# Slot 2 scored in one fp32 product from q and k as loaded, with a new list of steps

## The chip, the cores and the metric

The kernel runs on one core of one Trainium2 chip. The metric is the device time of one execution in microseconds (us). A core has TensorE (PE in the profile; its weight loads are PEld), VectorE (DVE), ScalarE (ACT), GpSimd (POOL) and SyncE (SP), which here issues every DMA.

## The reference

Two layers. The first is attention over 8 batches, 8 heads, 576 positions and head size 64, with a bias that falls with the running sum of `s`; the second is a mixture of 4 attention experts, of which each position takes the 2 with the largest gate.

```python
scores = scale * q @ k.T                       # per batch and head
cum = cumsum(maximum(s, 0))
scores = where(causal, -1e9, scores + minimum(-(cum_q - cum_k), 0))
attn = softmax(scores);  x = attn @ v          # heads side by side: x is [8, 576, 512]
logits = x @ w_gate                            # the top 2 of 4 experts, softmax of the two logits
for e in range(4):
    a = softmax(causal(scale * (x @ wq[e]) @ (x @ wk[e]).T))
    out += gate[e] * (a @ (x @ wv[e]) @ wo[e])
```

## The kernel before

The work is cut into slots numbered 0 to 49; a slot is one pair of heads (first layer) or one pair of experts (second layer) of one batch. Slots 0 to 3 are the four pairs of heads of batch 0. The keys of a slot lie on the partitions of the score banks and the queries on the columns, so each slot computes transposed scores `p[k, q]` for two heads.

Steps of a slot n, by the letters of the list (the number before the colon in the list is the slot at which the step is registered, so that a step on slot n's inputs stands under n-1 or n-2):

- `ld` loads q and k of a pair to a tile `raw` (L566, L576 for v as `lv`). `h0`..`h3` (L670, L674, ACT) copy them to fp32r tiles Q2 and K2; `lq`, `lk` make second copies (L689 POOL and L698 ACT in the first slots, DMAs later); `l0`..`l3` (L705, L711, DVE) store what the rounding to fp32r left over. `hc` (L632, L663) puts the running sums into rows 64 and following of the keys.
- `m0`..`m5` (L730, PE) compute a bf16 version of the scores, `M0`..`M5` (L744, DVE) reduce it to a row maximum per query; `M4` is the last. `mt` (L764, PE) turns the maxima, `mA` (L768, ACT) negates them, `mq` (L773, two DMAs, one for each head) writes them as row 96 of the queries. After that row has landed the true scores can be taken: the product itself subtracts the maximum.
- `s0`..`s6` are the scores (PE), `E0`..`E6` the exponentials (ACT), `b` the causal edges and `d` the sums (POOL), `v` the product with v (PE, L908), `a` and `r` the denominators, `n`, `N`, `o` the normalisation, `p` the projections of the second layer (PE, L1138).

An ordinary slot needs two fp32r products for each piece of its scores: the first with the rounding remainders (K1 and Q1, L798), the second with the rounded values, the sums and the maxima (K2 and Q2, L803). The slots in `DIRECT` (0 and 1) take another way: q and k are loaded by DMA into a tile `plain` without any rounding (`h0`, `h1`, L635 and L636), the rows beside them are set by memsets (`z0`, `z1` on DVE, `z2`, `z3` on POOL), and each piece is one fp32 product (L792, the tail L830), which the trace shows as two instructions. These slots need no `ld`, no `h2`, `h3` and no `l` steps.

The order on every engine is written out by hand in `ORDER` (L64), a list of 3951 steps; nothing moves at run time except by waiting. All DMAs go through SP's queue in that order. The list also has 60 spare products `i` (L1381): bf16 matmuls on a tile of zeros, whose results nobody reads. Forty of them stand at the very start of PE and twenty between the turn of slot 0's maxima (`-1:mt`) and slot 0's first scores.

Of the kernel before, what the change touches and what calls it, by code (L numbers as in the profile page):

```python
# [8 lines left out]
F32 = mybir.dt.float32  # L9
# [30 lines left out]
def pieces(kt, q0, q1):  # L40
# [302 lines left out]
def tile_attention_then_moe(ctx, tc, qk, vm, vt, s, wqk, wvg, wo, out):  # L343
# [244 lines left out]
    def r2(n):  # L588
        return n % NQK2
# [895 lines left out]
```

## Time and profile before

| | |
|---|---|
| median of 3 runs | 652.89 us (650.82 to 654.0) |
| the profiled execution | 653.66 us |
| its span, first to last instruction | 651.9 us |
| PE busy | 639.9 us, 98% of the span |
| DVE, ACT, POOL busy | 514.0, 467.4, 414.4 us |
| mean granted TensorE clock | 0.988 of full speed |

The page gives one execution. "Busy" is the time in which an engine has an instruction in work; matmuls overlap, so the start of the next matters more than the length of one. A granted clock of 1.00 stands for 2.4 GHz and 0.50 for 1.2 GHz.

### The profile page before, as it was taken

The page shows a single profiled execution, that of the slowest core. Times are in us where ns is not written, and L with a number is a line of the kernel's source. Part 1 is how long each engine was busy: PE and PEld are TensorE (multiplying, and loading weights), DVE is VectorE, ACT ScalarE, POOL GpSimd, SP SyncE. Part 2 cuts the span into 40 slices and gives each one's busy share as a digit, 9 for nine tenths or more (in the row PEclk, how much of TensorE's full clock was granted, in tenths as well). Part 3 has the DMA queues.
Part 4 walks back from the last instruction along what each step waited for, and adds up shares of the span by engine and source line. Part 5 has one row for each costly group of instructions (what it writes and reads, how often), then busy time and mean ns, then how long its engine had stood idle before and what let it go on. Part 6 is the DMA issues. An engine that isn't in the chain of part 4 may idle for free.

```text
span 651.9 us, 16521 instructions
## 1 busy us (share of the span) xinstructions
PE 639.9 (98%) x5891; PEld 529.3 (81%) x5891; DVE 514.0 (79%) x1459; ACT 467.4 (72%) x1077; POOL 414.4 (64%) x558
## 2 busy tenths in 40 slices
PE   7999999999999999999999999999999999999997
PEld 3377798888887898888888888878987888889875
DVE  7587978996888768988778788888778867874894
ACT  5268978777768767777677767777587866576564
POOL 9298567676756585675594758638765669837030
PEclk9699999999999999999999999999999999999999
DMA  7433553452547446264464346553445725232313
GB/s 169 138 111 102 154 144 103 134 136 62 148 112 182 104 129 170 72 179 140 125 170 136 120 95 166 146 145 109 112 129 157 203 61 129 59 110 73 95 45 114
DMA packets 49559, 81.29 MB, mean 125 GB/s; under 512 B 19892, under 2 KB 19892, under 8 KB 49478
## 3 DMA queue, kind: packets, MB, share of 16 engines
q1 hardware_dynamic: 49478, 80.24, 46.4%
q8 instruction: 47, 0.77, 0.5%
q14 instruction: 34, 0.28, 0.1%
HBM read 44.61 MB, written 10.16 MB: 84 GB/s over the span
## 4 chain that ended last, share of the span: by engine, by line
PE 92%; DMA 3%; ACT 2%; DVE 1%; SPq 1%; issue 1%; ACTq 0%; DVEq 0%
PE pvp L908 20%; PE pq L1138 16%; PE s L798 11%; PE s L803 10%; PE mx L730 10%; PE pw L1138 9%; PE po L1138 7%; PE sm L961 4%; DMA raw<-in_qk_dram 2%; PE s L792 2%; PE i L1381 1%; PE s L839 1%; PE po L1112 1%; PE mt L764 1%; ACT p L819 1%
## 5 line engine op out<-in xcount | busy, mean ns | idle before, releaser
L744 DVE CUSTOM_DVE_ANT_0 sink<-mx,mask 128x64 bf16<-128x64 f32 (+7 forms) x432 | 169.5, 428 | 56.2 <-PE mx L730 41.4
L819 ACT ACTIVATE p<-s 128x512 f32<-128x512 f32 x288 | 160.4, 593 | 52.1 <-PE s L803 40.0
L851 POOL TENSOR_SCALAR_AFFINE_SELECT p<-p 128x256 f32<-128x256 f32 (+1 forms) x192 | 95.4, 506 | 142.0 <-ACT p L819 117.0
L798 PE MATMUL s<-q,k 128*128 128x320 f32 (+2 forms) x552 | 149.7, 297 | 0.0
L803 PE MATMUL s<-q,k 97*128 97x320 f32 (+2 forms) x552 | 141.4, 290 | 1.3 <-DMA q<-mr 1.3
L872 POOL TENSOR_TENSOR r<-r,p 128x640 f32<-128x640 f32 (+1 forms) x92 | 128.6, 1399 | 4.3
L798 PEld LDWEIGHTS s<-q,k 128*128 128x128 f32 x552 | 105.0, 190 | 7.8 <-issue 4.0
L803 PEld LDWEIGHTS s<-q,k 97*128 97x128 f32 x552 | 105.0, 190 | 2.2 <-DMA q<-mr 1.5
L1138 PE MATMUL pq<-x,wqkh 128*128 128x288 f32 x512 | 106.2, 300 | 0.0
L908 PE MATMUL pvp<-p,v 128*64 128x128 f32 (+3 forms) x1024 | 99.9, 321 | 0.0
L705 DVE TENSOR_TENSOR q<-raw,q 64x576 fp32r<-64x576 f32 x92 | 78.7, 870 | 25.2 <-ACT q L670 9.0
L711 DVE TENSOR_TENSOR k<-raw,k 64x1024 fp32r<-64x1024 f32 (+1 forms) x92 | 82.7, 913 | 13.7 <-PE s L798 6.0
L730 PE MATMUL mx<-k,q 96*64 96x512 bf16 (+7 forms) x920 | 86.3, 293 | 1.0 <-ACT p L844 1.0
L1138 PEld LDWEIGHTS pq<-x,wqkh 128*128 128x128 f32 x512 | 81.5, 188 | 2.5 <-ACT pv L922 1.0
L908 PEld LDWEIGHTS pvp<-p,v 128*64 128x64 f32 x1024 | 63.7, 136 | 23.3 <-issue 3.0
L1138 PE MATMUL pq<-x,wqkl 128*128 128x288 f32 x256 | 75.5, 295 | 0.0
L670 ACT ACTIVATE q<-raw 64x576 fp32r<-64x576 f32 x92 | 62.0, 678 | 6.3 <-DMA raw<-in_qk_dram 5.1
L674 ACT ACTIVATE k<-raw 64x128 fp32r<-64x128 f32 (+1 forms) x92 | 61.8, 680 | 5.2 <-DMA raw<-in_qk_dram 3.1
L730 PEld LDWEIGHTS <-q 96*64 96x64 bf16 x920 | 45.0, 110 | 19.7 <-issue 6.2
L867 POOL TENSOR_TENSOR r<-p 128x256 f32<-128x256 f32 x46 | 37.4, 812 | 34.1 <-ACT p L819 34.1
L869 POOL TENSOR_TENSOR r<-p 128x384 f32<-128x384 f32 x46 | 49.2, 1070 | 11.3 <-ACT p L819 11.2
L922 ACT ACTIVATE pv<-pvp 128x256 f32<-128x256 f32 (+1 forms) x92 | 36.5, 402 | 25.4 <-PE pvp L908 25.1
(146 smaller groups left out, 1162.8 us busy)
## 6 DMA issues: line engine op xcount, KB each, us to landing
raw<-in_qk_dram SPq DMA_DIRECT2D x30, 576.0 KB
rb<-rr SPq DMA_DIRECT2D x92, 144.0 KB
q<-q SPq DMA_DIRECT2D x45, 288.0 KB
k<-k SPq DMA_DIRECT2D x39, 288.0 KB
v<-in_vm_dram SPq DMA_DIRECT2D x32, 256.0 KB
out_dram<-o SPq DMA_DIRECT2D x32, 256.0 KB
q<-mr SPq DMA_DIRECT2D x92, 2.2 KB
plain<-in_qk_dram SPq DMA_DIRECT2D x4, 288.0 KB
```

The lines of the kernel that those rows point to most:

```text
L670: nc.scalar.activation(q2[0:64, j], get_raw(n)[0:64, j], AF.Copy)
L705: nc.vector.tensor_tensor(a[64:128, j], get_raw(n)[0:64, j], q2[0:64, j].bitcast(F32), op=OP.subtract)
L711: nc.vector.tensor_tensor(part(c[0:64]), get_raw(n)[64:128, :, k], part(c[64:128]).bitcast(F32), op=OP.subtract)
L730: nc.tensor.matmul(t[64 * j : 64 * j + 64, c0 : c0 + k1 - k0], q2[0:RC, 64 * qt : 64 * qt + 64], keys(n, RC, j, k0, k1).bitcast(BF16)[:, 1 ...
L744: nc.vector.tensor_tensor_reduce(sink[:, c0 : c0 + w], t[:, c0 : c0 + w], mask[:, m0 : m0 + w], scale=1.0, scalar=mcol[n][:, 9:10] if bi = ...
L798: nc.tensor.matmul(t[0:nk, c0 : c0 + q1 - q0], K1[r1(n)][:, span(j, k0, k0 + nk)], Q1[r1(n)][:, j, q0:q1], start=True, stop=False,)
L803: nc.tensor.matmul(t[0:nk, c0 : c0 + q1 - q0], K2[r2(n)][0 : RM + 1, span(j, k0, k0 + nk)], Q2[r2(n)][0 : RM + 1, j, q0:q1], start=False, ...
L819: nc.scalar.activation(ptile[n][:, x % 2, 512 * ci : 512 * ci + 512], tl[x], AF.Exp, scale=0.125)
L851: nc.gpsimd.affine_select(out=a if kt else running()[:, :, 0:128], in_=a, pattern=[[64 if kt == 4 else 0, 2], [1, nk]], compare_op=OP.is_g ...
L872: add(r[:, :, q0:S], r[:, :, q0:S], p[:, :, 1024 + c : 1024 + c + S - q0], op=OP.add)
L908: nc.tensor.matmul(cur[h][64 * j : 64 * j + 64, q0 - PVC[h] : q1 - PVC[h]], vsl(j, kt), rtile[n][:, j, 0:128] if own else ptile[n][:, j, c ...
L1138: nc.tensor.matmul(t[0:nk, 0:w], l, r, start=(x == 0), stop=(x == len(terms) - 1))
```

## The change

`DIRECT` grows from (0, 1) to (0, 1, 2). Slot 2's q and k get a tile each, of the tag `raw2`: the two buffers in which later the projections leave the experts' q and k. Its `hc` copies the sums from the early table in SBUF instead of the table in DRAM. Nine steps go (`-1:ld`; `0:h2`, `0:h3`; `1:lq`, `1:lk`, `1:l0` to `1:l3`), four memsets come (`0:z0` to `0:z3`), and `0:h0`, `0:h1` turn from ACT copies into DMAs.

```diff
-DIRECT = (0, 1)
+DIRECT = (0, 1, 2)
...
     def whole(n):
-        if n not in plain:
+        if n not in plain and n < 2:
             w = sb.tile([P, 2, 4, S], F32, tag="x", name="plain", bufs=1)
-            for x, m in enumerate(DIRECT):
-                plain[m] = w[:, x]
+            for m in range(2):
+                plain[m] = w[:, m, 0:2], w[:, m, 2:4]
+        elif n not in plain:
+            plain[n] = tuple(
+                sb.tile([P, 2, S], F32, tag="raw2", name=f"plain{x}", bufs=2) for x in "qk"
+            )
         return plain[n]
...
-                nc.sync.dma_start(whole(n)[64:66, 2 + j], early[0][hd : hd + 1, 0:2])
+                nc.sync.dma_start(whole(n)[1][64:66, j], early[0][hd : hd + 1, 0:2])
...
-        items["h0"] = lambda: nc.sync.dma_start(whole(n)[0:64, 0:2], heads[0:64])
-        items["h1"] = lambda: nc.sync.dma_start(whole(n)[0:64, 2:4], heads[64:128])
+        items["h0"] = lambda: nc.sync.dma_start(whole(n)[0][0:64], heads[0:64])
+        items["h1"] = lambda: nc.sync.dma_start(whole(n)[1][0:64], heads[64:128])
```

The memsets and the other readers of the tile change their indices in the same way. The list itself is new throughout: of the 3942 steps that both lists have, the longest common run in order has 958. The start of both lists, cut to the steps of one engine (`i x40` for forty spare products):

```
PE before   i x40 | -2:m0 -2:m1 -2:m2 -1:m5 -1:m3 0:m5 0:m3 0:m4 -1:m0 -1:m1 -1:m2 -1:m4 -1:mt | i x20 | 0:s5 0:s4 ...
PE after    i x40 | -2:m0 -1:m3 -2:m2 -2:m1 -1:m1 0:m3 -1:m5 -1:m0 0:m5 0:m4 -1:m4 -1:m2 i -1:mt | i x19 | 0:s0 0:s1 ...
DVE before  -2:z1 -2:z0 -1:z0 -2:c2 -2:c3 2:l2 -2:c4 2:l0 -2:M0 -2:M1 -2:M2 -1:M5 -1:M3 -1:M4 ...
DVE after   -1:z0 -2:z1 -1:z1 -2:c2 -2:c3 -2:c4 0:z1 2:w0l -2:z0 -2:M0 -2:M1 -2:M2 -1:M5 -1:M3 -1:M4 ...
ACT before  1:h2 -2:c1 1:h0 2:lk 0:h3 0:h2 1:lk 0:h1 0:h0 2:w0h -1:mA ...
ACT after   -2:c1 2:w0h 2:lk 5:w0h 1:h2 2:h2 2:h3 2:h1 -1:mA ...
SP before   0:ld -2:c0 -2:h1 -1:h0 -2:h0 -1:ld -2:hc -1:h1 -1:hc 2:w0f -2:cu 1:ld -1:mq ...
SP after    -2:c0 -1:h0 2:w0f -2:h1 5:w0f -2:h0 0:ld -1:hc -2:hc -1:h1 1:ld -2:cu 0:hc 0:h0 2:ld 3:w0f -1:mq ...
```

Here `c0` loads `s`, `c1` to `c4` make the running sums (`c1` on ACT, the scan `c2` and the splits `c3`, `c4` on DVE), `cu` stores them to DRAM with four DMAs, and `w0f`, `w0h`, `w0l` load a weight and split it.

## Rows read from the trace of the kernel before

**Rows 1.** The page's head: the span, the busy times of the engines, and the shares of the engines in the chain that ended last.

```profile
span 651.9 us, 16521 instructions
PE 639.9 (98%) x5891; PEld 529.3 (81%) x5891; DVE 514.0 (79%) x1459; ACT 467.4 (72%) x1077; POOL 414.4 (64%) x558
PE 92%; DMA 3%; ACT 2%; DVE 1%; SPq 1%; issue 1%; ACTq 0%; DVEq 0%
```

**Rows 2.** All waits of PE from 60 us to the end (waiting line, releaser, us in total, times, longest).

```profile
PE mx L730 <- ACT p L844: 1.0, 1, 1.0
PE sm L1059 <- DVE r L872: 0.3, 1, 0.3
```

**Rows 3.** PE's timeline of the first 60 us: start, length, line, operation, count, and in brackets the idle time before it.

```profile
1.35 10.72 PE L1381 MATMUL i<-sink 128*128 128x512 bf16 x40 [1.35 <-DVE sink L373]
12.60 0.36 PE L730 MATMUL mx<-plain 96*64 96x448 bf16 x1 [0.53 <-DVE p L473]
13.25 1.23 PE L730 MATMUL mx<-plain 96*64 96x448 bf16 x17 [0.29 <-DMA plain<-p]
16.33 3.04 PE L730 MATMUL mx<-plain 96*64 96x256 bf16 x22 [1.86 <-DMA w_qk<-in_wqk_dram]
20.32 0.37 PE L764 MATMUL mt<-ident,mcol 128*9 128x128 f32 x1 [0.94 <-DVE mcol L744]
20.48 9.52 PE L1381 MATMUL i<-sink 128*128 128x512 bf16 x20
29.89 5.60 PE L792 MATMUL s<-plain 128*128 128x320 f32 x24
35.33 0.27 PE L764 MATMUL mt<-ident,mcol 128*9 128x128 f32 x1
...
38.36 3.72 PE L792 MATMUL s<-plain 128*128 128x256 f32 x16
...
47.23 0.42 PE L798 MATMUL s<-q,k 128*128 128x320 f32 x1
...
50.38 0.34 PE L839 MATMUL s<-q,k 128*128 128x128 f32 x2
50.65 0.43 PE L730 MATMUL mx<-k,q 96*64 96x320 bf16 x4
...
56.67 0.31 PE L798 MATMUL s<-q,k 128*128 128x320 f32 x1
58.30 0.42 PE L803 MATMUL s<-q,k 97*128 97x320 f32 x1 [1.31 <-DMA q<-mr]
```

**Rows 4.** Windows of the start: from and to in us, their length, busy us (and instructions) of PE, PEld, DVE, ACT, POOL, the granted clock, the DMA engines' busy share and GB/s.

```profile
5.00:10.00 5.00, 5.00 (x24) 2.23 (x23) 2.72 (x4) 3.17 (x5) 4.70 (x18) 1.00 1.04 204
...
14.00:15.00 1.00, 0.47 (x8) 0.16 (x2) 1.00 (x5) 0.99 (x3) 0.87 (x3) 1.00 0.69 237
15.00:16.00 1.00, 0.00 (x0) 0.00 (x0) 1.00 (x9) 0.99 (x2) 1.00 (x2) 0.75 0.59 194
...
25.00:29.00 4.00, 3.99 (x10) 1.43 (x10) 0.32 (x1) 0.00 (x0) 0.00 (x0) 0.50 0.76 236
```

**Rows 5.** DVE's timeline of the start (columns as in rows 3): the running sums and their two splits, the first and the last maxima of slot 0.

```profile
7.32 1.35 DVE L457 TENSOR_TENSOR_SCAN s_c<-s_r 64x576 f32<-64x576 f32 x1 [2.21 <-ACT s_r L452]
8.70 1.05 DVE L463 TENSOR_SCALAR p<-s_c 64x576 int32<-64x576 int32 x1
9.78 0.75 DVE L469 TENSOR_TENSOR p<-s_c,p 64x576 f32<-64x576 f32 x1
...
11.84 0.75 DVE L473 TENSOR_TENSOR p<-p 64x576 f32<-64x576 f32 x1
...
13.79 0.62 DVE L744 CUSTOM_DVE_ANT_0 sink<-mx,mask 128x448 bf16<-128x448 f32 x1 [0.42 <-POOL plain L640]
...
16.69 0.69 DVE L744 CUSTOM_DVE_ANT_0 sink<-mx,mask 128x512 bf16<-128x512 f32 x1
...
19.41 0.75 DVE L744 CUSTOM_DVE_ANT_0 sink<-mx,mask,mcol 128x512 bf16<-128x512 f32 x1 [2.02 <-PE mx L730]
```

**Rows 6.** SP's issues in the same stretch (start, time that the issuing took, line, transfer, count).

```profile
2.62 1.26 SPq L635 DMA_DIRECT2D plain<-in_qk_dram  x2
...
10.63 1.45 SPq L632 DMA_DIRECT2D plain<-p  x2
12.13 0.67 SPq L636 DMA_DIRECT2D plain<-in_qk_dram  x1
...
21.01 1.64 SPq L773 DMA_DIRECT2D plain<-mr  x2
```

**Rows 7.** The chain that ended last, in order of time: two of its DMA pieces (start, length).

```profile
0.81 5.10 DMA raw<-in_qk_dram
...
54.33 3.92 DMA q<-mr
```

**Rows 8.** Groups of instructions of the first 60 us (count, busy us, mean ns of one, idle time before them).

```profile
L711 DVE TENSOR_TENSOR k<-raw,k 64x1024 fp32r<-64x1024 f32 (+1 forms) x6 | 5.6, 958 | 0.1
L670 ACT ACTIVATE q<-raw 64x576 fp32r<-64x576 f32 x8 | 5.4, 676 | 3.9 <-DMA raw<-in_qk_dram 3.8
...
L705 DVE TENSOR_TENSOR q<-raw,q 64x576 fp32r<-64x576 f32 x6 | 4.7, 786 | 0.2
...
L638 DVE MEMSET plain<- 32x1152 f32 x2 | 2.0, 1018 | 0.6 <-DVE q L705 0.3 <-issue 0.3
```

More of the change, by code (lines that the diff above doesn't have):

```diff
@@ L608, in whole @@
     def whole(n):
-        if n not in plain:
+        if n not in plain and n < 2:
             w = sb.tile([P, 2, 4, S], F32, tag="x", name="plain", bufs=1)
-            for x, m in enumerate(DIRECT):
-                plain[m] = w[:, x]
+            for m in range(2):
[4 more added lines that the diff above has]
+            )
         return plain[n]
     def queries(n):
-        return whole(n)[:, 0:2] if n in DIRECT else Q2[r2(n)]
+        return whole(n)[0] if n in DIRECT else Q2[r2(n)]
     def keys(n, rows, j, k0, k1):
         if n in DIRECT:
-            return whole(n)[0:rows, 2 + j, k0:k1]
+            return whole(n)[1][0:rows, j, k0:k1]
         return K2[r2(n)][0:rows, span(j, k0, k1)]
@@ L631, in sums_in @@
                 hd = 2 * i + j
-                nc.sync.dma_start(whole(n)[64:66, 2 + j], early[0][hd : hd + 1, 0:2])
+                nc.sync.dma_start(whole(n)[1][64:66, j], early[0][hd : hd + 1, 0:2])
         items["hc"] = sums_in
-        items["h0"] = lambda: nc.sync.dma_start(whole(n)[0:64, 0:2], heads[0:64])
-        items["h1"] = lambda: nc.sync.dma_start(whole(n)[0:64, 2:4], heads[64:128])
-        items["z0"] = lambda: nc.vector.memset(whole(n)[64:96, 0:2], 1.0)
-        items["z1"] = lambda: nc.vector.memset(whole(n)[96:128, 0:2], 0.0)
-        items["z2"] = lambda: nc.gpsimd.memset(whole(n)[64:96, 2:4], 0.0)
-        items["z3"] = lambda: nc.gpsimd.memset(whole(n)[96:128, 2:4], 1.0)
+        items["h0"] = lambda: nc.sync.dma_start(whole(n)[0][0:64], heads[0:64])
+        items["h1"] = lambda: nc.sync.dma_start(whole(n)[1][0:64], heads[64:128])
+        items["z0"] = lambda: nc.vector.memset(whole(n)[0][64:96], 1.0)
+        items["z1"] = lambda: nc.vector.memset(whole(n)[0][96:128], 0.0)
+        items["z2"] = lambda: nc.gpsimd.memset(whole(n)[1][64:96], 0.0)
+        items["z3"] = lambda: nc.gpsimd.memset(whole(n)[1][96:128], 1.0)
         return items
```

512 rows, old and new, of the table ORDER are left out of this document.

## The prediction

> **What bounds the kernel now.** I read the page's head first: PE is busy for 98% of the span and holds 92% of the chain that ended last [rows 1]. So the question is where PE is not doing needed work. Two views answer it. PE's waits after 60 us come to 1.0 + 0.3 = 1.3 us in all [rows 2]: from there on the time is the sum of PE's work. PE's timeline of the start shows the rest [rows 3]. Slot 0's first true product starts at 29.89, and before it PE does 40 spare products (1.35 to 12.07), the maxima of slots 0 and 1 (12.60 to about 19.4), the turn of the maxima at 20.32 and 20 more spares, which take from 20.48 to about 30. So the needed stream begins at 29.89, and from there it stands still only once, 1.31 us at 58.30. The time is therefore the start of that stream, plus the length of its work, plus its few waits, plus what follows it.
>
> The reader should see one thing more: the twenty spares are slow. At full clock 24 fit into 5 us, 0.208 each [rows 4]; these took 9.52/20 = 0.476 [rows 3]. The granted clock fell between 15 and 16 us (0.75 on the mean of that microsecond, 0.50 later, that is 1.2 for 2.4 GHz) after PE had stood at 12.07 to 12.60, at 13.0 to 13.25 and from 14.48 on [rows 3, 4]. It was still at 0.50 from 25 to 29.
>
> The profiled execution took 653.66 us, 1.76 more than its span and 0.77 more than the median. I work out differences on the span and carry them to the median of 652.89.
>
> **The fp32 product: dearer on PE.** Slot 0's 24 instructions at L792 run from 29.89 to slot 1's turn at 35.33: 5.44 us. Slot 2's pairs of L798 and L803 run from 47.23 to the tail at 50.38: 3.15 us [rows 3]. Slot 2 changes from the second to the first: +2.29. The tail (0.27 before, 50.38 to 50.65) becomes four smaller instructions; that lies between -0.27 and +0.27, and I take 0. The maxima read another tile at the same number of columns, 72 ns each on `plain` (1.23/17); I take 0. All of this lies on PE where nothing else hides it: **+2.3 us**.
>
> Row and rule: the Trainium skill (FP8 and Floating Point Precision, TensorE Precision Notes) says that a true fp32 product takes four passes through the array. An estimate from that: 3072 columns times four at 2.4 GHz is 5.1 us, and the reduced form in two products half of it, a price of 2.6. The trace's 2.29 agrees in kind and is the one used.
>
> **What goes from the other engines.** Off go four ACT copies of `h` and two of `lk` (about 0.68 each [rows 8]), two POOL copies, and on DVE two L705 and two L711, 2 x 0.79 + 2 x 0.96 = 3.5 us. On come two DVE memsets (2.0) and two on POOL. All of this ran before 30 us in the old list, where PE had spares, and later PE was never short of work [rows 2]; I count it at nothing by itself. It matters only through the start, which the new list orders anew.
>
> **The start, step by step.**
>
> The 40 spares stand first in both lists and end at 12.07. DVE: the scan stood 2.21 us for ACT and began at 7.32 [rows 5], so DVE was free at 5.1. ACT now has the running sums first and SP loads `s` first, no longer behind a 576 KB load. Scan at 5.1; from its start to the end of the first split it is 9.78 + 0.75 - 7.32 = 3.2, so 8.3 (before 10.53). Then `c4` (about 1.2, of which 0.75 in its row), a memset (1.02 [rows 8]), a weight's low part (about 0.7, as a 512-column reduction [rows 5]) and `-2:z0` (1.02) with some 0.3 of gaps: 12.5. So slot 0's maxima start at 12.5 as before at 12.60.
>
> What is late next is slot 1's k. SP waits for the first split, now 8.4, then issues two pairs of `hc` at 1.45 [rows 6] and `-1:h1` at 11.3; before, at 12.13. Before, PE got at the maxima of slot 1 at 16.33, 4.2 later; a small load was used 2.0 after its issue (10.63 to 12.60). Between these, I take 3.0: 14.3. Meanwhile PE has four banks of slot 0 instead of three things to do: 16 x 0.072 = 1.2, to 13.7. It stands until 14.3 and does the other 24 in 1.7 at full clock (3.3 at the rate of 16.33, 3.04/22).
>
> DVE's reductions of slot 0 begin at about 13.2. Five of them took 13.79 to 17.38 and the last 0.75 [rows 5]; now nothing holds the last one for 2.02 us if slot 1's k lands by 14.3. They end at 17.6, and with k at 15.5 at 18.5. I take the turn at **18.0, before 20.32**.
>
> The row of the maxima: ACT has three copies of slot 4's `raw` ahead of `-1:mA`. That load is issued at 12.0; the 576 KB load of the start took 5.10 beside others [rows 7], so it is there by 17.1, three copies take 2.0, `mA` 0.3, and `-1:mq` is issued at 19.4. It lands 2.0 to 3.9 later (the quickest small load above, and the slowest in the chain [rows 7]): 21.4 to 23.3.
>
> The spares: 19 instead of 20 behind the turn. All at full clock: 18.0 + 0.15 + 19 x 0.208 = 22.1. All slow: 18.15 + 19 x 0.476 = 27.2. Here is the main unknown, for the trace has no row of the new pattern. PE now stands less before 15.5 (0.4 and 0.6 instead of 0.5, 0.3 and 1.85), which speaks for the clock; but it then has only one spare between the last maxima at 16.0 and the turn at 18.0, which speaks against it. I take half of them slow: 18.15 + 9 x 0.476 + 10 x 0.208 = **24.5**, later than the row's landing. Gain at the start: 29.89 - 24.5 = **5.4**.
>
> A second rule speaks against the list: on each DMA engine, descriptors are taken in the order of the ring (the Trainium skill, DMA: Bandwidth & Descriptors, Queues, rings and completion order). `0:h0`, `2:ld` and `3:w0f` (288 + 576 + 256 KB) now stand ahead of `-1:mq`; the rows show no such case at the start. At the 204 GB/s of the start 1.15 MB take 5.6 us, an estimate: from about 17 to 22.6, later than 21.4 and within the bounds above, so only a fast clock would feel it.
>
> **The rest of the list.** Slot 1's first product now follows its turn by 20 maxima of slot 2 (1.45), the tail and four pieces of pv, in sum about 2.7, where it was 38.36 - 35.33 = 3.0 without a stall; I take a wait of **0.4** (0 to 1.3, the stall at 58.30). Beyond, the new list can win at most 1.3 at 58.30 and 1.3 later; it can lose a few. I add the PE steps between turn and first product over all slots, at the spacings of rows 3: the shortest are 3.2 us before and, slot 1 apart, 3.2 after. So I take 0, with -2.5 to +4.
>
> **Sum.** -5.4 + 2.3 + 0.4 = -2.7: 652.89 - 2.7 = **650.2**.
>
> **The rivals.**
>
> - *The clock holds.* Then the row's landing decides, 22.1 to 23.3, say 22.6: -7.3 + 2.7 = -4.6, 648.3. For it: the shorter stands before 15.5. Against it: the gap before the turn.
> - *All spares slow.* 27.2: -2.7 + 2.7 = 0, 652.9. The start gains just what the fp32 product costs. For it: the old trace, where the clock stayed at 0.50 for over 13 us although spares were running [rows 4].
> - *The new list waits in the stream.* The row of a slot's maxima lands as late as 3.92 after it was issued [rows 7], and the shortest distances between turn and product are 3.2. Each such wait costs PE the 1.3 seen at 58.30. Starting from 652.9 it ends slower by 0.5% with three of them beyond the old one; with three or four, 657.5. For it: PE has no other slack. Against it: in the old list, with distances as short, it happened once in 50 slots.
>
> **How the numbers follow.** Half slow 0.40, clock holds 0.25, all slow 0.22, waits 0.13. A measurement of this kernel can tell about 0.5% from no change, 3.3 us: faster is below 649.6, slower above 656.2. The forecast's own range is 648 to 652.5, of which a bit over 0.4 lies below 649.6; of the clock's case 0.8, of the slow one 0.05 or so: 0.17 + 0.20 + 0.01, and a little for a gain from the list, gives 0.40 faster. Slower is most of the waits' case and a few hundredths of the slow one: 0.14. The rest, 0.46, is no change. The range takes in the clock's case with a list that wins 2.5 (645.8) and the slow case with one that loses 2.9 (655.8); above lies only the waits' case.
>
> **What would show it.** The 24 instructions of slot 2 at L792 in 5.4 us; the turn `-1:mt` at 17.6 to 18.5; the granted clock between 15 and 25 us, and with it the time of the 19 spares (4 to 9 us); the start of `0:s0` at 22 to 27.5; PE's waits after 60 us near 1.3. The prediction is wrong if slot 0's first product doesn't come before 28, if slot 2's products cost other than 2.3, or if PE waits several times on the row of the maxima.

## The result: slower by 0.7%

The changed kernel takes 656.48 us (median of 6 runs) against 652.31 for the kernel before on the same chip: ratio 1.0066, 95% interval [1.0046, 1.0087]. That is 4.3 us slower, where 2.7 us faster was forecast. The profile below is of an execution of 658.16 us, 1.7 over the median.

### The profile after

In the changed kernel the line numbers of the steps are 4 higher (L798 is L802, L744 is L748), in most experiments 5 higher. First the page's head, as in [rows 1].

```profile
span 656.1 us, 16578 instructions
PE 642.7 (98%) x5893; PEld 529.4 (81%) x5893; DVE 521.5 (79%) x1457; ACT 464.6 (71%) x1071; POOL 412.6 (63%) x558
PE 86%; DMA 5%; DVE 3%; ACT 2%; SPq 1%; POOL 1%; issue 1%; POOLq 0%; DVEq 0%; ACTq 0%
```

PE still looks 98% busy, which hides the loss. The chain of waits shows it better: PE's share fell from 92% to 86%, DVE's and DMA's rose. And DVE's busy time *rose* by 7.5 us, although the change took four remainders from it and brought only two memsets (2.0 us): the remainders got longer. Those of q, over the whole execution (count, busy us, mean ns of one), in the kernel before and in the changed one:

```profile
L705 DVE TENSOR_TENSOR q<-raw,q 64x576 fp32r<-64x576 f32 x92 | 78.7, 870 | 25.2 <-ACT q L670 9.0
L709 DVE TENSOR_TENSOR q<-raw,q 64x576 fp32r<-64x576 f32 x90 | 84.9, 959 | 23.6 <-ACT q L674 12.9
```

PE's timeline of the first 52 us, as in [rows 3]:

```profile
...
13.45 1.24 PE L734 MATMUL mx<-plain 96*64 96x448 bf16 x14 [1.98 <-DVE plain L641]
14.93 3.31 PE L734 MATMUL mx<-plain 96*64 96x384 bf16 x26 [0.25 <-DMA plain<-in_qk_dram]
...
19.07 0.42 PE L768 MATMUL mt<-ident,mcol 128*9 128x128 f32 x1
19.34 7.46 PE L1385 MATMUL i<-sink 128*128 128x512 bf16 x19
26.69 5.42 PE L796 MATMUL s<-plain 128*128 128x256 f32 x24
...
44.62 4.58 PE L796 MATMUL s<-plainq,plaink 128*128 128x320 f32 x20
49.05 0.27 PE L768 MATMUL mt<-ident,mcol 128*9 128x128 f32 x1
...
50.36 1.13 PE L796 MATMUL s<-plainq,plaink 128*128 128x320 f32 x4
51.42 0.34 PE L834 MATMUL s<-plainq,plaink 128*64 128x64 f32 x4
```

The start is better, as forecast: slot 0's first product begins at 26.69 instead of 29.89. Slot 2's fp32 products take 49.05 - 44.62 = 4.43 and 51.42 - 50.36 = 1.06, together 5.49 instead of 3.15: the forecast +2.3. So at 52 us the changed kernel is about 0.9 us ahead. It ends 4.2 us behind. Those 5 us went in the stream, which [rows 2] showed to be almost without waits. All of PE's waits after 60 us now:

```profile
PE mt L768 <- DVE mcol L748: 1.4, 1, 1.4
PE pvp L912 <- DVE mcol L748: 0.8, 1, 0.8
PE mx L734 <- DVE mcol L748: 0.7, 1, 0.7
PE s L802 <- DVE mcol L748: 0.7, 2, 0.4
PE s L843 <- DMA q<-mr: 0.5, 1, 0.5
PE s L843 <- DVE k L715: 0.5, 1, 0.5
```

4.6 us instead of 1.3, and 4.1 of them end with DVE: with its maxima (`mcol`) or with a remainder of k (L715). All lie between 213 and 400 us. The largest stretch not explained by a late DMA is at 320 us. DVE there (start, length, instruction):

```profile
315.64 4.26 DVE L709 TENSOR_TENSOR q<-raw,q 64x576 fp32r<-64x576 f32 x1
319.93 0.75 DVE L748 CUSTOM_DVE_ANT_0 sink<-mx,mask,mcol 128x512 bf16<-128x512 f32 x1
...
320.72 1.22 DVE L715 TENSOR_TENSOR k<-raw,k 64x1024 fp32r<-64x1024 f32 x1
...
321.98 0.69 DVE L748 CUSTOM_DVE_ANT_0 sink<-mx,mask 128x512 bf16<-128x512 f32 x1
```

POOL at the same time:

```profile
315.63 0.46 POOL L878 TENSOR_TENSOR r<-r,p 128x128 f32<-128x128 f32 x1
316.05 1.57 POOL L876 TENSOR_TENSOR r<-r,p 128x640 f32<-128x640 f32 x1
317.59 0.73 POOL L869 TENSOR_TENSOR r<-p 128x256 f32<-128x256 f32 x1
318.29 1.00 POOL L876 TENSOR_TENSOR r<-r,p 128x384 f32<-128x384 f32 x1
319.36 0.86 POOL L878 TENSOR_TENSOR r<-r,p 128x128 f32<-128x128 f32 x1
```

And the two waits of PE that follow:

```profile
320.84 0.44 PE L912 MATMUL pvp<-r,v 128*64 128x128 f32 x4 [0.79 <-DVE mcol L748]
...
322.73 0.42 PE L734 MATMUL mx<-k,q 96*64 96x384 bf16 x4 [0.69 <-DVE mcol L748]
```

The reader is to see this: a remainder of q, 0.75 us of work, took 4.26 us. It started 0.01 us after a POOL add, POOL then issued one add behind the other, and the remainder ended 0.6 after the fourth of them (319.29). The reductions queued behind it came late, and PE waited. Length alone need not cost anything: in the kernel before the longest remainder of q took 2.12 us (at 593.8) and one of k 2.46 (at 377.7), and PE waited for neither [rows 2]. The theory to be tested (theory 1): the list, not the fp32 product, loses the 5 us, because in its middle DVE's remainders stand beside POOL's trains of adds and ahead of reductions that PE soon needs.

The Trainium skill (SBUF — State Buffer, Who interferes with whom) has a rule for such pairs: a DVE instruction with two inputs in SBUF shares a read interface with GpSimd instructions that read SBUF, the one that starts first holds it for its whole length, and the other waits. A remainder has two such inputs. The trace agrees that it waits, and shows more than this rule says: the remainder ended 3.5 us late, behind the fourth of four POOL instructions and not behind the first.

### The profile page after: what moved, and what is told of

The parts are those of the page before. It is cut to its first block, busy times and chain, and to the rows that moved or that the text cites. A ratio compares the mean times of both kernels' runs of the same rounds, so it can differ in the third digit from the quotient of the medians.

```text
span 656.1 us, 16578 instructions
## 1 busy us (share of the span) xinstructions
PE 642.7 (98%) x5893; PEld 529.4 (81%) x5893; DVE 521.5 (79%) x1457; ACT 464.6 (71%) x1071; POOL 412.6 (63%) x558
## 4 chain that ended last, share of the span: by engine, by line
PE 86%; DMA 5%; DVE 3%; ACT 2%; SPq 1%; POOL 1%; issue 1%; POOLq 0%; DVEq 0%; ACTq 0%
PE pvp L912 19%; PE pq L1142 14%; PE s L802 10%; PE s L807 9%; PE mx L734 9%; PE pw L1142 8%; PE po L1142 6%; PE sm L965 4%; PE s L796 2%; DMA k<-k 1%; PE s L843 1%; PE i L1385 1%; DVE sink L748 1%; DVE k L715 1%; PE po L1116 1%; DMA rb<-rr 1%
## 5 line engine op out<-in xcount | busy, mean ns | idle before, releaser
L748 DVE CUSTOM_DVE_ANT_0 sink<-mx,mask 128x64 bf16<-128x64 f32 (+7 forms) x432 | 169.0, 428 | 44.9 <-PE mx L734 32.1
L855 POOL TENSOR_SCALAR_AFFINE_SELECT p<-p 128x256 f32<-128x256 f32 (+1 forms) x192 | 96.8, 513 | 123.2 <-ACT p L823 100.5
L802 PE MATMUL s<-q,k 128*128 128x256 f32 (+2 forms) x540 | 146.3, 297 | 0.8 <-DVE mcol L748 0.7
L807 PE MATMUL s<-q,k 97*128 97x256 f32 (+2 forms) x540 | 138.4, 290 | 0.0
L876 POOL TENSOR_TENSOR r<-r,p 128x640 f32<-128x640 f32 x92 | 124.4, 1353 | 5.1
L802 PEld LDWEIGHTS s<-q,k 128*128 128x128 f32 x540 | 102.8, 190 | 8.3 <-issue 3.7
L709 DVE TENSOR_TENSOR q<-raw,q 64x576 fp32r<-64x576 f32 x90 | 84.9, 959 | 23.6 <-ACT q L674 12.9
L807 PEld LDWEIGHTS s<-q,k 97*128 97x128 f32 x540 | 102.7, 190 | 0.9 <-DMA q<-mr 0.4
L715 DVE TENSOR_TENSOR k<-raw,k 64x1024 fp32r<-64x1024 f32 (+1 forms) x90 | 84.1, 945 | 15.3 <-PE s L802 7.2
L674 ACT ACTIVATE q<-raw 64x576 fp32r<-64x576 f32 x90 | 60.6, 678 | 7.1 <-DMA raw<-in_qk_dram 4.1
L873 POOL TENSOR_TENSOR r<-p 128x384 f32<-128x384 f32 x46 | 51.9, 1129 | 20.5 <-ACT p L823 20.4
L678 ACT ACTIVATE k<-raw 64x128 fp32r<-64x128 f32 (+1 forms) x90 | 60.2, 680 | 2.6 <-ACT xt L1040 0.8
L926 ACT ACTIVATE pv<-pvp 128x256 f32<-128x256 f32 (+1 forms) x92 | 36.8, 407 | 27.6 <-PE pvp L912 26.6
```

The source lines that it names most:

```text
L674: nc.scalar.activation(q2[0:64, j], get_raw(n)[0:64, j], AF.Copy)
L709: nc.vector.tensor_tensor(a[64:128, j], get_raw(n)[0:64, j], q2[0:64, j].bitcast(F32), op=OP.subtract)
L715: nc.vector.tensor_tensor(part(c[0:64]), get_raw(n)[64:128, :, k], part(c[64:128]).bitcast(F32), op=OP.subtract)
L748: nc.vector.tensor_tensor_reduce(sink[:, c0 : c0 + w], t[:, c0 : c0 + w], mask[:, m0 : m0 + w], scale=1.0, scalar=mcol[n][:, 9:10] if bi = ...
L802: nc.tensor.matmul(t[0:nk, c0 : c0 + q1 - q0], K1[r1(n)][:, span(j, k0, k0 + nk)], Q1[r1(n)][:, j, q0:q1], start=True, stop=False,)
L807: nc.tensor.matmul(t[0:nk, c0 : c0 + q1 - q0], K2[r2(n)][0 : RM + 1, span(j, k0, k0 + nk)], Q2[r2(n)][0 : RM + 1, j, q0:q1], start=False, ...
```

## The experiments

The list is cut at the turns of slots, which stand in both lists; "the turn of slot 14" is the step `14:mt`. In the changed kernel the cuts lie at 75 us (`5:mt`), 190 (`14:mt`), 280 (`21:mt`) and 378 (`28:mt`). All ratios are to the kernel before, timed on the same chip. (Of the 3942 steps that both lists have, at most 1267 stand in the same order, not 958.)

**The old list with the new code.**

```diff
 DIRECT = (0, 1, 2)
-ORDER: new list
+ORDER: old list; 0:h0 0:h1 for -1:ld, 0:z2 ahead of -1:z3, 0:z3 for 1:lq, 0:z0 for 1:l2, 0:z1 for 1:l0
```

> The changed code (slot 2 in one fp32 product, its buffers) under the old list; the steps that the change drops are left out, and the six new ones stand where the steps of that kind stood. In the changed kernel slot 2's products took 5.49 us against 3.15 before, and TensorE lost about 5 us in waits and stretched steps between 213 and 400 us. Theory 1 (the new list's order between 200 and 400 us costs those 5 us, the code only the 2.3): 2.3 us over the kernel before, ratio 1.003 to 1.005. Rival 2 (the code itself, the fp32 product and the buffers it takes, sets off the late waits): as slow as the changed kernel or slower, ratio 1.007 to 1.012.

Measured: 1.0035 [1.0018, 1.0052], +2.3 us (1.2 to 3.4). The code costs the fp32 price, as far as this interval can tell; the rival that the code sets off the waits falls. In its profile slot 0's first product begins at 28.54 instead of 29.89 although the turn is as late as before (20.40): the same 20 spares took 8.08 us instead of 9.52, because the clock was back at 26.3 and not at 29.1. More on that below.

**New start, old order behind it.**

```diff
-ORDER: new list
+ORDER: new list to 5:mt, old list behind it
```

> The changed code with the new list up to slot 5's turn (75 us in the changed kernel), and from there the old order. Theory 1: the start's gain of 3.2 us against slot 2's 2.3 is kept and the late loss goes: 0.9 us under the kernel before, ratio 0.997 to 1.000. Rival 2 (code) or a rival in which the new start itself shifts what is late afterwards: as the changed kernel, ratio 1.005 to 1.009.

Measured: 1.0024 [1.0005, 1.0042]. A miss for both: better than the changed kernel, but only 0.7 us better than the old list, which is within the noise. In the profiles its first product is 1.5 us ahead of the old list's (27.07 and 28.54), and one wait of 1.5 us for an exponential, which no other profile has, takes that back.

**Old start, new order behind it.**

```diff
-ORDER: new list
+ORDER: old list to 5:mt, new list behind it
```

> The changed code with the old list up to slot 5's turn, and from there the new order. Theory 1: no gain at the start, slot 2's 2.3 us and the late 5 us: 7 us over the kernel before, ratio 1.009 to 1.013. Rival (the stalls come from the new start running ahead of its loads): they go with the old start, ratio 1.003 to 1.005.

Measured: 1.0125 [1.0093, 1.0156], 8.2 us slower. As theory 1 has it, and the long remainder comes back at the same place, with other starts of everything (the same step, on DVE's timeline):

```profile
317.45 4.25 DVE L710 TENSOR_TENSOR q<-raw,q 64x576 fp32r<-64x576 f32 x1
```

4.26 and 4.25 us, and 4.26 once more in the first of the two kernels with half of the middle old, below: a property of the order, not the luck of an execution. The largest single wait of the changed kernel, 1.4 us at 297 behind a DMA that took 8.69 us, does not come back here, nor in any other profile: that one was luck.

**New list, its middle in the old order.**

```diff
-ORDER: new list
+ORDER: new list to 14:mt, old list to 28:mt, new list behind it
```

> The new list, with the steps from slot 14's turn to slot 28's (190 to 378 us in the changed kernel) in the old order, and the new order before and behind. Theory 1 puts 4 to 5 us of the loss in that stretch: 1 us over to 1 us under the kernel before, ratio 0.998 to 1.002. Rival (the loss moves with the work, wherever the order is tight): ratio 1.004 or more.

Measured: 0.9996 [0.9978, 1.0013]. The old middle gives back 0.70%, 4.6 us. The windows of that middle stretch show what PE did in it (from and to, length, then busy us and instructions of PE, PEld, DVE, ACT, POOL, clock, DMA share, GB/s). The changed kernel:

```profile
189.70:378.20 188.50, 184.26 (x1727) 154.10 (x1724) 156.03 (x429) 136.13 (x315) 120.66 (x155) 1.00 0.50 133
```

The same stretch with the old order:

```profile
188.50:370.10 181.60, 181.60 (x1720) 152.71 (x1717) 149.93 (x428) 135.91 (x313) 118.80 (x155) 1.00 0.51 137
```

188.5 us became 181.6, with almost the same instructions on all engines. PE had 4.2 us without work and now has none; DVE is busy 6.1 us less with one instruction less. (Of PE's other 2.7 us, 0.9 is work that the two orders put on different sides of the cut: behind it PE is busy 273.1 and 274.0 us.)

**POOL's long adds cut short, under both lists.**

```diff
                 _, q0, _, c = SCHUNKS[2][x - 3]
+                if 13 <= n <= 28:
+                    p = p[:, :, 1024 + c : 1024 + c + 16]
+                    add(r[:, :, q0 : q0 + 16], r[:, :, q0 : q0 + 16], p, op=OP.add)
+                    return
```

(To keep the sums that are left away from zero, the constant added to them is 1.0 in both.)

> The changed kernel with GpSimd's two long running adds of slots 13 to 28 cut to 16 of their columns; part of those slots' row sums is left out. It is to be held against the same cut under the list whose middle is old (e6). Theory 1, in the form that GpSimd's adds stretch VectorE's remainder operations and these come late: the 4.26 us remainder at 315 us takes about 0.75 us, TensorE's waits on the columns of maxima go, and the run stands within 1.5 us of e6: ratio to before 0.997 to 1.002. Rival (the distances in the new order and the late landings do it, without any stretch): 3.5 us or more over e6, ratio 1.004 to 1.008.

> The same cut of the adds of slots 13 to 28 in the list with the old middle; the same part of the row sums is left out. With the old middle there was no wait of TensorE on these operations, so both theories expect little: 0 to 1.5 us under the kernel with the old middle, ratio to before 0.996 to 1.000.

Measured: 1.0035 [1.0017, 1.0052] under the new list, 0.9995 [0.9973, 1.0016] under the one with the old middle. In the first, the long remainder (on DVE's timeline) and all of PE's waits after 60 us are:

```profile
313.21 0.92 DVE L709 TENSOR_TENSOR q<-raw,q 64x576 fp32r<-64x576 f32 x1
```

```profile
PE s L802 <- DVE mcol L748: 0.4, 1, 0.4
PE s L807 <- DMA q<-mr: 0.3, 1, 0.3
PE mx L734 <- ACT p L823: 0.3, 1, 0.3
```

4.26 became 0.92, and the waits on `mcol` went from 3.6 (1.4 of them the one at 297 us) to 0.4: the mechanism is shown at this place. Only these two adds are shorter, and nothing else was moved. But the time fell by only 0.31%, 2 us, just clear of the noise, and 2.6 us stay between the two cut kernels, more than the 1.5 that theory 1 allowed and less than the 3.5 of its rival: a miss for both.

PE's turns tell where the cut works. From slot 21's turn to slot 28's PE took 98.2 us in the changed kernel, 95.4 with the adds cut and 93.8 with the old middle; from slot 14's to slot 21's 90.3 with full and with cut adds, and 87.8 with the old middle. In that first half a remainder of k at 213 us did fall from 1.54 us to 0.29, and the two waits behind it went, but others of 0.3 us came. And one place did not change at all: a remainder of k beside a short add and two causal edges, which were not cut, took 1.81 us for 1.22 in both kernels, with the same wait of PE behind it. The changed kernel, then the one with cut adds:

```profile
249.16 1.81 DVE L715 TENSOR_TENSOR k<-raw,k 64x1024 fp32r<-64x1024 f32 x1
252.57 0.41 PE L802 MATMUL s<-q,k 128*128 128x320 f32 x1 [0.37 <-DVE mcol L748]
```

```profile
248.30 1.81 DVE L715 TENSOR_TENSOR k<-raw,k 64x1024 fp32r<-64x1024 f32 x1
251.71 0.42 PE L802 MATMUL s<-q,k 128*128 128x320 f32 x1 [0.37 <-DVE mcol L748]
```

That all of the rest is of this kind is not shown.

**One remainder moved.**

```diff
-23:M0 24:l0 23:mq 24:s0 24:h2 24:p2 25:m3 24:m3 22:d5 24:v3 24:M4 23:l1 24:M3 24:v0
+23:M0 23:mq 24:s0 24:h2 24:p2 25:m3 24:m3 22:d5 24:v3 24:M4 23:l1 24:M3 24:l0 24:v0
```

> The changed kernel with one single step moved: slot 24's remainder of q for one head (the operation that took 4.26 us at 315.6 us beside GpSimd's unbroken train of adds, and 4.25 us with the old start) goes behind the reductions of banks 4 and 3 that it held up. Theory 1: the remainder takes 0.75 us or little more there, TensorE's stretched and waiting stretches of 1.03 and 0.99 us at 319.6 and 321.1 go: 1.5 to 2.2 us under the changed kernel, ratio to before 1.003 to 1.005. Rival (the order's distances, so that the next thing is late in their place): no gain, 1.006 to 1.008.

Measured: 1.0054 [1.0034, 1.0073], between the two ranges, 0.8 us under the changed kernel where 1.5 to 2.2 were expected; the intervals overlap, so the time alone doesn't show a gain. The stretch from slot 21's turn to slot 28's does: 95.8 us in this profile, 97.2 to 98.2 in the three that have it in the new order with nothing moved or cut. What happened there (DVE):

```profile
315.38 2.60 DVE L716 TENSOR_TENSOR k<-raw,k 64x1024 fp32r<-64x1024 f32 x1 [1.33 <-PE s L803]
...
318.74 0.75 DVE L710 TENSOR_TENSOR q<-raw,q 64x576 fp32r<-64x576 f32 x1
```

The moved remainder took its 0.75, and the next one, of k, inherited the train: 2.60 instead of 1.22.

**The two halves of the middle.**

```diff
-ORDER: new list
+ORDER: new list to 14:mt, old list to 21:mt, new list behind it   (second kernel: 21:mt and 28:mt)
```

> The new list with the old order from slot 14's turn to slot 21's only (190 to 280 us in the changed kernel). In the profiles this stretch takes 90.3 us with the new order, with the full or the cut adds alike, and 87.8 with the old. Theory 1 (each half has its own late operations, which only add up): 1.5 to 2.5 us under the changed kernel, ratio 1.003 to 1.005. Rival (only the train of adds at 315 us and its neighbours cost anything): no gain, 1.006 to 1.008.

> The new list with the old order from slot 21's turn to slot 28's only (280 to 378 us). The profiles: 98.2 us with the new order, 95.8 with one remainder moved, 95.4 with the adds cut, 93.8 with the old order. Theory 1: 2.5 to 4 us under the changed kernel, ratio 1.000 to 1.003. Rival (what the second half gains, the stretch behind it gives back): 1.004 or more.

Measured: 1.0042 [1.0024, 1.0060], in the range of theory 1, and 1.0033 [1.0009, 1.0058], just above it and under its rival's. Against 1.0066 that is 0.24% for the first half and 0.33% for the second, 0.57% of the 0.70% that both give; either alone is not clear of the noise. The profiles separate them: the first half takes 87.8 to 89.0 us in the ten profiles that have it in the old order and 89.25 to 90.8 in the five that have it in the new; the second 93.6 to 94.9 in ten, and 97.2 to 98.2 in the three with the new order untouched. Behind slot 28's turn these two kernels take 277.8 and 278.0 us, the changed one 277.9. So the cost is spread over both halves, and what one gains is not given back behind it.

**The start: `s` first under the old code and list.**

```diff
-  -2:i34 0:ld -2:f12 -2:f22 -2:z2 -2:i9 1:h2
+  -2:i34 -2:c0 0:ld -2:f12 -2:f22 -2:z2 -2:i9 -2:c1 1:h2
```

> The kernel before, code and list, with one change: the load of s goes ahead of slot 0's raw load on its queue, and its activation ahead of the one before it on ScalarE. If the scan (7.32 us before, 5.13 in the changed kernel) is what sets the first turn: scan near 5.1, the turn at 18.2 to 19.3 in place of 20.32, 1 to 2 us less in all, ratio 0.997 to 0.999. Rival (the loads of slot 0's plain q and k set it, which now come half a microsecond later): 0 to 0.6 us more, ratio 1.000 to 1.001.

Measured: 0.9973 [0.9952, 0.9994], 1.8 us less, as expected, with the scan at 5.14 us and the turn at 17.88. Two steps moved in the old list give 2.4 us at the turn without the fp32 product and without a new list.

**Fewer spares behind the turn**, first in the new list with the old middle (11 for 19), then on the kernel just named (12 and 6 for 20). The first edit:

```diff
-SPARE = 60
+SPARE = 52
-ORDER: -1:mt, 19 spares, 0:s0
+ORDER: -1:mt, 11 spares, 0:s0
```

> The list with the old middle and 8 fewer spare products behind the first turn, 11 in place of 19 (52 in all). In that kernel's profile the turn is at 18.68 us, the spares run to 25.69 and the first row of maxima is issued at 19.28. If the spares only fill the time until the row lands: slot 0's first product at 23 to 23.7 us, 2 to 2.5 us less in all, ratio to before 0.995 to 0.998. Rival (the spares are what brings the clock back, which stood at half until 24 us): slot 0's 24 products run at half speed in part, nothing gained or up to 3 us lost, ratio 0.999 to 1.004.

> The kernel before with s loaded first, and 8 of the 20 spares behind the first turn taken out (52 in all). There the turn came at 17.9, the 20 spares ran to 26.5 at 0.43 us each on average, the clock was back at 24.5. If the spares only fill: 12 of them at 0.55 to 0.6 us end at 24.6 to 25.2, 1.3 to 1.9 us less than with 20: ratio to before 0.994 to 0.996. Rival (the clock comes back later for want of spares): 0.997 to 0.999.

> The same with 14 of the 20 taken out (46 in all). The 6 left end near 21.5, the second row of maxima lands near 22, and slot 0's products begin at the lower clock; if the clock is back at 24.5 as with 20 spares, they have then done 1.2 us of their work: 3 us less than with 20 spares, ratio to before 0.992 to 0.994. Rival (a TensorE that waited gets its clock back later, and slot 0's 24 products take up to 5 us longer): 0.997 to 1.003.

Measured: 0.9983 [0.9964, 1.0002]; **0.9934 [0.9912, 0.9956]**; 0.9933 [0.9909, 0.9958]. The first is in neither range, 0.8 us under the kernel with the old middle and within the noise: its 11 spares all ran at the lower clock, 0.56 us each, and slot 0's first product came at 25.06 instead of 25.69. The other two, at 647.27 and 647.61 us, are 4.3 us better than the kernel before and, by the ratios, 8.6 better than the changed one; the second is better than either range, the third in the first of its two. PE's timelines, with 20, 12 and 6 spares:

```profile
17.99 8.61 PE L1382 MATMUL i<-sink 128*128 128x512 bf16 x20
26.48 5.60 PE L793 MATMUL s<-plain 128*128 128x320 f32 x24
```

```profile
17.29 5.52 PE L1381 MATMUL i<-sink 128*128 128x512 bf16 x12
22.70 5.60 PE L792 MATMUL s<-plain 128*128 128x320 f32 x24
```

```profile
17.75 3.37 PE L1381 MATMUL i<-sink 128*128 128x512 bf16 x6
21.23 7.53 PE L792 MATMUL s<-plain 128*128 128x320 f32 x24
```

With 6 spares the products begin 1.5 us earlier than with 12 and run 1.9 longer, for the clock is not yet back (0.54 on the mean from 18 to 25 us). So 8 fewer spares gave 2.5 us (0.9973 to 0.9934), and the next 6 nothing: spares behind the landing of the row of maxima were lost time here.

## Why the prediction was wrong

- **The fp32 product: right.** +2.29 was forecast, 5.49 - 3.15 = 2.34 is what the trace has, and the old list with the new code costs +2.3 us by the measured ratio (1.2 to 3.4).
- **"The rest of the list ... So I take 0, with -2.5 to +4": this step failed.** It cost 4.6 us, by the kernel with the old middle. I judged the new order by one distance, from a slot's turn to its first product, because the only stall of the old trace [rows 2] was a late row of maxima. I did not look at DVE's queue, where a remainder and a reduction stand in a row, or at what POOL does beside it. [rows 8] gave the remainders of the first 60 us as 0.79 and 0.96 us on average; that those of q average 0.87 over the whole trace of the kernel before, where a quick one takes 0.75, and that this can grow, was not asked. In place of 0 the runs show 4.6 us in the middle of the list: about 2 of them go when POOL's two long adds are cut, and with them the longest held-up remainder; how the rest comes about stays open.
- **The start: right in kind, too large.** A gain of 5.4 was forecast; the profile has 3.2, and the eight profiled kernels with the new start and all its spares have slot 0's first product between 25.6 and 27.3 instead of 24.5. Some 1.4 us of the 3.2 look like bad luck of the profile before: the two kernels with the old start and the new code, with the turn as late (20.4) and the same 20 spares, have it at 28.5, not at 29.89, because their clock came back at 26.3 and 26.1 and not at 29.1. Two terms were off. The scan came at 5.13 as forecast, but the turn at 19.07 instead of 18.0, because `c4` and the memset behind it ended later (DVE; `c4`'s first part took 1.39 where I had about 0.45):

```profile
7.87 1.39 DVE L463 TENSOR_SCALAR p<-p 64x576 int32<-64x576 int32 x1
...
12.38 1.02 DVE L641 MEMSET plain<- 32x1152 f32 x1 [0.29 <-issue]
```

  And the 19 spares took 7.35 instead of 6.4. The clock (last column but two) stood at half until 24 us:

```profile
14.00:15.00 1.00, 0.75 (x12) 0.32 (x10) 0.97 (x5) 0.01 (x1) 0.96 (x2) 0.64 1.00 283
...
19.00:24.00 5.00, 4.66 (x11) 1.05 (x10) 4.26 (x6) 3.19 (x6) 1.33 (x2) 0.50 0.74 218
24.00:25.00 1.00, 1.00 (x5) 0.47 (x4) 0.00 (x0) 0.00 (x0) 0.00 (x0) 0.74 1.04 238
```

  The chain that ended last counts 13 spares from 23.18 on (start, length, count):

```profile
23.18 3.62 PE i L1385 x13
```

  So the six before took 23.18 - 19.34 = 3.84, 0.64 each at half clock. That half of the spares would be slow was right: 10 of the 19 began before the clock was back at 24.5. Their price was not: the 0.476 of [rows 3] was itself a mean, of seven at 0.64, ten near 0.42 and three at 0.22. The 2.0 us of a small load were read at a product that [rows 3] show waiting for DVE; nothing hung on that, since the spares ended (26.69) behind the latest landing of the row that was forecast (23.3).
- **The wait of slot 1 (0.4):** none came; no wait of PE is recorded between 26.69 and 213 us.
- **The sum.** By the measured ratios: +2.3 for the product (old list, new code), -2.6 for the start and all else (new list with the old middle, at -0.3 in all), +4.6 for the middle: +4.3, what was measured; each term is uncertain by 1 us or more, and the second is what the measured -0.3 leaves beside the first. The forecast had +2.3, -5.0 and 0.
- **The rivals.** "The new list waits in the stream" had the sign and the place, at 657.5 against 656.5, but another cause: the row of the maxima accounts for 0.5 of the 4.6 us of waits. "Wrong if PE waits several times on the row of the maxima" would not have fired. "All spares slow" came nearer to the time of the first product (27.2 against 26.69) than the half I chose, though half is what were slow.

Open: with POOL's long adds cut, 2.6 us stay between the new middle and the old. PE's recorded waits are then 1.0 us against 0.2, so some 1.8 us lie inside PE's busy time, most of them between the turns of slots 14 and 21. A part is how a wait is counted: the next product starts some 0.15 us before the end given for the one ahead of it (slot 2's 20 products run to 49.20, the turn starts at 49.05), so a wait costs that much more than its idle time, about 0.3 us for three waits against one. The rest no run here names.

## What to carry to other kernels

When a hand-written order is replaced, check it on every engine's queue, not only on the bound one: an engine at 79% can stop one at 98% if a stretched instruction stands ahead of one that is needed soon. Ask of each long mean in a group whether it is work or waiting; a group of equal instructions between 0.75 and 4.26 us is waiting in part, and the neighbouring engine's timeline in the same window says for whom. What it costs is decided by what stands behind it in the queue. And when a change mixes an edit with a new order, try the parts alone: here two moved steps and eight spares less in the old list gave 4.3 us, while the fp32 product cost 2.3 and the new middle 4.6. A single profile of a start that hangs on the clock is one draw: here it was 1.4 us off.

## What was not expected of the hardware

- A DVE instruction with two SBUF inputs was held by a train of POOL instructions until the end of the fourth of them, 4.26 us for 0.75, and in the same way (4.25 and 4.26) in two other lists. Cutting the two long adds brought it to 0.92.
- The clock's fall at the start is not the same between kernels with the same list up to there: the changed kernel was at half from 14.3 to 24.5 us, the one with the old middle (the same list up to 190 us) only from 20.2 to 23.6. In the eight profiles with the new start and all its spares the clock fell between 14.3 and 20.7 and came back between 23.4 and 26.6. In single profiles its return does not follow the number of spares either. Windows of the kernels with 12 and then 6 spares (columns as above):

```profile
18.00:22.00 4.00, 3.67 (x9) 0.90 (x8) 3.60 (x6) 1.97 (x3) 3.02 (x3) 0.60 0.06 19
22.00:23.00 1.00, 1.00 (x4) 0.43 (x3) 0.80 (x2) 0.00 (x0) 0.00 (x0) 0.88 0.89 241
```

```profile
18.00:25.00 7.00, 6.62 (x15) 3.43 (x14) 6.53 (x18) 3.01 (x5) 2.10 (x2) 0.54 0.39 115
25.00:26.00 1.00, 1.00 (x5) 0.83 (x5) 0.93 (x7) 0.60 (x1) 0.24 (x1) 0.84 0.69 192
```

  With 12 the clock is back soon after 22 us, with 6 soon after 25, and with 20 at 24.8 (0.60 on the mean from 24 to 25).
- The first seven spares behind a turn stand further apart than the later ones, at either clock: in the kernel with the old middle 0.43 us before the clock fell at 20.2, then 0.64 until 22.1; from there 0.43, and 0.22 after the clock's return at 23.6.
